# Attention softmax: 1e-9 added to the sums of both heads in one instruction

## The chip, the cores and the metric

The kernel runs on one core of a Trainium2 chip. The metric is the device time of one execution in microseconds (us). A core has five engines with a queue each: TensorE (PE, matrix products; its weight loads are the row PEld), VectorE (DVE), ScalarE (ACT), GpSimd (POOL) and SyncE (SP, which issues transfers). Each works through its queue in order, and they wait for each other by semaphores.

## What is computed

The program is threshold attention followed by a Fourier mixing layer with a two-layer network. The change lies in the attention, for 8 batches of 8 heads with 576 positions of 64 values:

```
scores = scale * q @ k.T
thresh = max(scores) - tau
scores = where(scores >= thresh, scores, -1e9)
attn = exp(scores - max(scores))
attn = attn / (sum(attn) + 1e-09)
out = attn @ v
```

Then, per batch, x is the 576 x 512 matrix of all heads' outputs; u is x plus the real part of its two-dimensional Fourier transform, and the result is u + relu(norm(u) @ w_ch1) @ w_ch2. All of it is in 32-bit floats.

## The kernel before

**Steps.** Two heads make a pair, and a pair is worked in five steps: steps t = 0 to 3 take 128 query rows of each of the two heads, and step t = 4 takes the last 64 rows of both heads together as one block of 128 rows. So a batch has 4 x 5 = 20 steps, the program 160; in 128 of them two blocks are normalized (nh = 2 in the code), in 32 one (nh = 1).

**One step.** `scores` (L431, or L437 for the last step of a pair) puts the products of queries and keys into two score banks `sc`, one for each head; the two banks of a tag rotate, so the next step's products wait for this step's last reader. `softmax` then does, with j as the head:

- L455, DVE: the negated maximum of each row into `neg`
- L463, ACT: exp(score - maximum) into `e`
- L467, ACT, behind the first exponential: the threshold `thr` for both heads
- L471, DVE: `e` times (score >= thr), the masking, which also sums each row into a column of `den`. In the trace it is two entries: the operation, and DVE_READ_ACCUMULATOR, which writes the sum
- L476, DVE: 1e-9 added to that column of `den`
- L485, DVE, after both heads: the inverse of `den`, both columns at once

In the first two batches a copy of the inverse is spread by POOL (L497) and the weighted values are multiplied by it later (L589); from the third batch on, DVE (L488) and ACT (L492) multiply `e` by it, one head each. `weights_in_parts` (L534, L537, L552) transposes `e` on TensorE, ACT copies the result out (L540, L554), and `weighted_values` (L581) multiplies it with v.

**Around it.** In the first 40 steps (two batches) the order of all engines is the order of the program text. In that stretch both weight matrices, given as 64-bit floats, are also loaded in pieces and converted to 32 bits, in stages that the steps call: L297, L300 and L312 on DVE, L305, L308 and L319 on ACT, L317 and L320 on POOL. The hooks `between` (behind the first head's masking; there `weighted_values` of the pair stands, with L589), `meanwhile` (behind the maxima) and `behind` (after both heads; the last conversion stage, on ACT and POOL) place this work inside a step. While little other work is ready, TensorE also runs warming products that feed nothing (`busy`, L112). From the third batch on (step 40) the text orders TensorE alone, and a scheduler orders the other engines.

Two-layer products (L814 and L840 for the first token groups, L918 and L1082 for the later ones), the Fourier products (L684, L701, L705) and their additions fill TensorE between the steps. After step 159, with the last attention done, only these remain.

Of the kernel before, what the change touches and what calls it, by code (L numbers as in the profile page):

```python
# [12 lines left out]
ALU = mybir.AluOpType  # L13
# [15 lines left out]
def _repeated(ap, n):  # L29

    return bass.AP(
        tensor=ap.tensor,
        offset=ap.offset,
        ap=[list(ap.ap[0]), list(ap.ap[1]), [0, n]],
    )
# [12 lines left out]
def kernel(  # L48
# [12 lines left out]
    nc = tc.nc  # L61
# [104 lines left out]
    for u in range(2):  # L166
# [14 lines left out]
        out=q_scale[:], in0=tau_t[:], scalar1=0.0, scalar2=SCALE, op0=ALU.is_ge, op1=ALU.mult  # L181
# [3 lines left out]
        out=below[:], in0=tau_t[:], scalar1=0.0, scalar2=-3.0e38, op0=ALU.is_lt, op1=ALU.mult  # L185
# [3 lines left out]
        out=tau_pos[:], in0=tau_t[:], scalar1=0.0, scalar2=-1.0, op0=ALU.max, op1=ALU.mult  # L189
# [226 lines left out]
    def normalized(n):  # L416


        return n >= 2 * NPAIR
# [23 lines left out]
    def softmax(i, between=None, meanwhile=None, behind=None):  # L443


        t = i % NT
        sc, nh = steps[i]
        neg = sb.tile([128, 2], FP32, tag="neg", bufs=3, name="neg")
        thr = sb.tile([128, 2], FP32, tag="thr", bufs=3, name="thr")
        den = sb.tile([128, 2], FP32, tag="den", bufs=3, name="den")  # L450


        e = sb.tile([128, 2 * S], FP32, tag="e", name="e")
        for j in range(nh):
            nc.vector.tensor_reduce(  # L455
                out=neg[:, j : j + 1], in_=sc[j][:, :, 0:HALF], axis=AXIS_XY, op=ALU.max,
                negate=True,
            )
        if meanwhile is not None:
            meanwhile()  # L460
        for j in range(nh):
            ej = e[:, S * j : S * (j + 1)].rearrange("p (c n) -> p c n", c=2)
            nc.scalar.activation(  # L463
                out=ej, in_=sc[j][:, :, 0:HALF], func=ACT.Exp, bias=neg[:, j : j + 1], scale=1.0
            )
            if j == 0:
                nc.scalar.activation(  # L467
                    out=thr[:, 0:nh], in_=neg[:, 0:nh], func=ACT.Identity,
                    bias=thr_off[:, :], scale=-1.0,
                )  # L470
            nc.vector.scalar_tensor_tensor(  # L471
                out=ej, in0=sc[j][:, :, 0:HALF], scalar=thr[:, j : j + 1], in1=ej,
                op0=ALU.is_ge, op1=ALU.mult, accum_out=den[:, j : j + 1],
            )

            nc.vector.tensor_scalar(  # L476
                out=den[:, j : j + 1], in0=den[:, j : j + 1], scalar1=1e-9, scalar2=None,
                op0=ALU.add,
            )
            if between is not None:  # L480
                between()
                between = None
        if behind is not None:
            behind()
        nc.vector.reciprocal(den[:, 0:nh], den[:, 0:nh])  # L485
        rec = None
        if normalized(i // NT):
            nc.vector.tensor_scalar(  # L488
                out=e[:, 0:S], in0=e[:, 0:S], scalar1=den[:, 0:1], scalar2=None, op0=ALU.mult
            )  # L490
            if nh == 2:
                nc.scalar.activation(  # L492
                    out=e[:, S : 2 * S], in_=e[:, S : 2 * S], func=ACT.Copy, scale=den[:, 1:2]
                )
        else:
            rec = sb.tile([128, 2 * D], FP32, tag="rec", name="rec")
            nc.gpsimd.tensor_copy(  # L497
                rec[:, :].rearrange("p (j d) -> p j d", j=nh), _repeated(den[:, 0:nh], 2 * D // nh)
            )
        if t == 4:  # L500
            nc.scalar.copy(e[:, S : S + 64], e[:, 512:S])
        steps[i] = (e, rec)
# [674 lines left out]
    def step(i):  # L1177
# [15 lines left out]
        if t == 1 and n > 0:  # L1193
            softmax(i, lambda: weighted_values(n - 1, 1), next_stages, last_stage)
            load_v(n + 1)
        elif t == 3:
            softmax(i, lambda: weighted_values(n, 0), next_stages, last_stage)
        else:
            softmax(i, None, next_stages, last_stage)
# [281 lines left out]
```

## Time and profile before

| what | value |
|---|---|
| time, median of three runs | 1632.56 us (1632.07 to 1632.69) |
| span of the profiled execution | 1631.3 us |
| busy PE, PEld | 1583.8 us (97%), 1248.7 us (77%) |
| busy DVE, ACT, POOL | 1173.4 us (72%), 817.8 us (50%), 659.3 us (40%) |
| mean granted TensorE clock | 0.994 of full speed |
| the additions L476 | 288, first at 13.7 us, last at 1431.0 us |
| the first normalization L488 (third batch) | 285.7 us |

A share of busy time is a mean over stages with different limits. The chain of work that ended last says more: it is followed back from the last instruction, at each step to what released it, or to the instruction ahead of it on its engine. In the groups of instructions, a line gives the source line, the engine, the operation, the tile written and those read, the shapes and the count, then the busy time in us and the mean of one in ns, then the engine's idle time just ahead of these and what ended it. In a timeline, a line begins with the start and the duration in us.

### The profile page before, as it was taken

To read this page: it belongs to the slowest core of one execution; us is meant where nothing else is said; L and a number is where in the kernel's file an instruction comes from. 1 tells how busy PE (TensorE), PEld (TensorE's weight loads), DVE (VectorE), ACT (ScalarE), POOL (GpSimd) and SP (SyncE) were. 2 spreads that over 40 slices of the span, in tenths; PEclk is the share of its full clock that TensorE was granted. 3 is DMA by queue.
4 is the path that set the end of the run, shared out by engine and by line. 5 is a ranking of instruction groups with operands and counts; after the bars stand their busy time and mean duration, and the time that the engine had idled before them with its cause. 6 is when DMAs were issued, how large, how long until landed. Compare 5 with 4: busy or idle time off the path is not lost.

```text
span 1631.3 us, 27898 instructions
## 1 busy us (share of the span) xinstructions
PE 1583.8 (97%) x10346; PEld 1248.7 (77%) x10346; DVE 1173.4 (72%) x2518; ACT 817.8 (50%) x1738; POOL 659.3 (40%) x875
## 2 busy tenths in 40 slices
PE   8998999999999999999999999999999999999998
PEld 4555655577887888878888778877878788889998
DVE  7997886667758686857576868786787869664445
ACT  5765665544455454645445546454636455523111
POOL 6784673042421452244342244224352344124332
PEclk9999999999999999999999999999999999999999
DMA  6423222101110101110011010111111110000000
GB/s 162 123 56 113 74 75 57 40 17 22 20 38 17 34 9 43 23 29 16 21 23 36 17 34 11 41 23 35 17 27 32 22 29 2 14 7 7 14 14 14
DMA packets 203084, 57.41 MB, mean 35 GB/s; under 512 B 193827, under 2 KB 193829, under 8 KB 202950
## 3 DMA queue, kind: packets, MB, share of 16 engines
q1 hardware_dynamic: 200438, 55.34, 14.5%
q8 instruction: 82, 1.34, 0.4%
q10 hardware_dynamic: 2512, 0.30, 0.1%
q14 instruction: 52, 0.43, 0.1%
HBM read 46.02 MB, written 9.44 MB: 34 GB/s over the span
## 4 chain that ended last, share of the span: by engine, by line
PE 77%; DVE 14%; ACT 4%; POOL 2%; issue 2%; DMA 1%; SPq 1%; DVEq 0%; ACTq 0%; POOLq 0%
PE ph L918 24%; PE po L1082 20%; PE pv L581 9%; PE sc L431 7%; PE pw L552 6%; PE po L840 3%; DVE neg L455 2%; DVE e L471 2%; PE ph L814 2%; PE sc L437 1%; ACT e L463 1%; PE pn L774 1%; PE py L684 1%; PE pa L701 1%; DVE hs L1043 1%
## 5 line engine op out<-in xcount | busy, mean ns | idle before, releaser
L463 ACT ACTIVATE e<-sc,neg 128x576 f32<-128x576 f32 x288 | 212.5, 738 | 224.7 <-DVE neg L455 224.5
L455 DVE TENSOR_REDUCE neg<-sc 128x1 f32<-128x576 f32 x288 | 207.3, 748 | 161.6 <-PE sc L431 149.7
L471 DVE SCALAR_TENSOR_TENSOR e<-sc,thr,e 128x576 f32<-128x576 f32 x288 | 229.4, 812 | 42.2 <-ACT thr L467 40.4
L1082 PE MATMUL po<-w,hs 128*128 128x256 f32 x1024 | 246.2, 383 | 0.0
L1082 PEld LDWEIGHTS po<-w,hs 128*128 128x128 f32 x1024 | 186.1, 190 | 33.8 <-issue 12.8
L918 PE MATMUL ph<-u_t,w 128*128 128x128 f32 x1536 | 188.1, 277 | 0.0
L431 PE MATMUL sc<-kT,qT 64*128 64x288 f32 x1024 | 174.4, 433 | 12.6 <-DVE e L471 11.1
L918 PEld LDWEIGHTS ph<-u_t,w 128*128 128x128 f32 x1536 | 180.2, 193 | 5.0 <-issue 3.7
L552 PE MATMUL pw<-ident,e 128*128 128x128 f32 x1152 | 170.7, 275 | 7.8 <-ACT y_o L689 2.3
L554 ACT COPY e_t<-pw 128x512 f32<-128x512 f32 x256 | 148.8, 594 | 48.9 <-PE pw L552 48.2
L927 DVE TENSOR_TENSOR hs<-ph,hs 128x512 f32<-128x512 f32 x160 | 106.9, 685 | 70.7 <-PE ph L918 54.0
L431 PEld LDWEIGHTS sc<-kT,qT 64*128 64x128 f32 x1024 | 96.0, 187 | 78.1 <-issue 37.5
L552 PEld LDWEIGHTS pw<-ident,e 128*128 128x128 f32 x1152 | 134.9, 141 | 27.2 <-ACT y_o L689 4.2
L918 PE MATMUL ph<-t_u,s_w 128*128 128x128 f32 x1024 | 126.7, 277 | 2.1 <-POOL t_u L892 1.8
L918 PEld LDWEIGHTS ph<-t_u,s_w 128*128 128x128 f32 x1024 | 119.9, 192 | 7.4 <-issue 4.6
L1082 PE MATMUL po<-hs,s_tile 128*128 128x256 f32 x512 | 121.5, 381 | 0.0
L796 DVE SCALAR_TENSOR_TENSOR u<-po,rstd,u 128x256 f32<-128x256 f32 (+1 forms) x164 | 75.3, 483 | 63.9 <-PE po L1082 62.8
L492 ACT ACTIVATE e<-e,den 128x576 f32<-128x576 f32 x96 | 74.6, 777 | 76.5 <-DVE den L485 76.0
L1082 PEld LDWEIGHTS po<-hs,s_tile 128*128 128x128 f32 x512 | 94.0, 190 | 13.7 <-issue 2.5
L935 ACT ACTIVATE hs<-hs 128x512 f32<-128x512 f32 x112 | 69.2, 630 | 61.6 <-DVE hs L927 61.6
L614 POOL TENSOR_TENSOR half<-x 128x287 f32<-128x287 f32 x48 | 40.5, 865 | 119.5 <-ACT x L587 61.1
L1078 POOL TENSOR_TENSOR hs<-hs,s_tile 128x512 f32<-128x512 f32 x32 | 42.0, 1314 | 107.9 <-PE po L1082 85.0
(194 smaller groups left out, 2899.5 us busy)
## 6 DMA issues: line engine op xcount, KB each, us to landing
hs<-in_moe_w_ch_dram SPq DMA_DIRECT2D x23, 512.0 KB, 4.8
q_in<-in_q_dram SPq DMA_DIRECT2D x128, 72.0 KB, 2.5
out_dram<-u SPq DMA_DIRECT2D x36, 256.0 KB, 2.2
k_in<-in_k_dram SPq DMA_DIRECT2D x124, 72.0 KB, 2.5
v_in<-in_v_dram SPq DMA_DIRECT2D x64, 128.0 KB, 2.4
w<-in_moe_w_ch_dram SPq DMA_DIRECT2D x6, 512.0 KB, 3.6
stage<-in_moe_w_ch_dram SPq DMA_DIRECT2D x3, 512.0 KB, 3.6
v_in<-in_v_dram SPq DMA_DIRECT2D x64, 16.0 KB, 2.2
```

The source lines that it names most:

```text
L431: nc.tensor.matmul(sc[j][:, c, 0:HALF], qT[hp, 128 * t : 128 * t + 128], kT[hp, k0 + HALF * c : k0 + HALF * (c + 1)], start=True, stop=True,)
L455: nc.vector.tensor_reduce(out=neg[:, j : j + 1], in_=sc[j][:, :, 0:HALF], axis=AXIS_XY, op=ALU.max, negate=True,)
L463: nc.scalar.activation(out=ej, in_=sc[j][:, :, 0:HALF], func=ACT.Exp, bias=neg[:, j : j + 1], scale=1.0)
L471: nc.vector.scalar_tensor_tensor(out=ej, in0=sc[j][:, :, 0:HALF], scalar=thr[:, j : j + 1], in1=ej, op0=ALU.is_ge, op1=ALU.mult, accum_out ...
L492: nc.scalar.activation(out=e[:, S : 2 * S], in_=e[:, S : 2 * S], func=ACT.Copy, scale=den[:, 1:2])
L552: nc.tensor.transpose(pw[:, c, :], e[:, c0 : c0 + 128], ident[:, :])
L554: nc.scalar.copy(e_t[:, 4 * j : 4 * j + 4, qs], pw[:, :, :])
L581: nc.tensor.matmul(pv[64 * j : 64 * j + 64, 0:m], vt[:, 2 * c + j, :], e_t[:, 4 * j + c, 0:m] if c < 4 else ends[:, 0, 0:m], start=(c == 0 ...
L796: nc.vector.scalar_tensor_tensor(out=u, in0=product, scalar=self.rstd[:, t : t + 1], in1=u, op0=ALU.mult, op1=ALU.add,)
L918: nc.tensor.matmul(banks[name][:, 128 * q : 128 * q + 128], left[c][:, 512 * part + 128 * q : 512 * part + 128 * q + 128], right[c], start ...
L927: nc.vector.tensor_tensor(out=to, in0=bank, in1=to if other is None else other, op=ALU.add)
L1082: nc.tensor.matmul(bank[:, 0 : DM // 2], left[p], right[p], start=start and p == 0, stop=p == NK - 1, skip_group_check=True,)
```

## The change

The two additions of 1e-9, one behind each head's masking, go. In their place one addition over all `nh` columns of `den` stands behind the hook `behind`, directly ahead of the inverse. It is for having one small instruction of DVE fewer in every step with two heads, and none between the maskings of the two heads. Steps with one head keep one addition.

```diff
@@ in softmax, inside the loop over the heads @@
                 out=ej, in0=sc[j][:, :, 0:HALF], scalar=thr[:, j : j + 1], in1=ej,
                 op0=ALU.is_ge, op1=ALU.mult, accum_out=den[:, j : j + 1],
             )
-
-            nc.vector.tensor_scalar(
-                out=den[:, j : j + 1], in0=den[:, j : j + 1], scalar1=1e-9, scalar2=None,
-                op0=ALU.add,
-            )
             if between is not None:
                 between()
                 between = None
         if behind is not None:
             behind()
+        nc.vector.tensor_scalar(
+            out=den[:, 0:nh], in0=den[:, 0:nh], scalar1=1e-9, scalar2=None, op0=ALU.add
+        )
         nc.vector.reciprocal(den[:, 0:nh], den[:, 0:nh])
```

## The prediction

> **What bounds the kernel now.** I read first the shares of busy time and the chain of work that ended last. TensorE is busy 97% of the span, and the chain says where that is the true bound:
>
> ```profile
> PE 77%; DVE 14%; ACT 4%; POOL 2%; issue 2%; DMA 1%; SPq 1%; DVEq 0%; ACTq 0%; POOLq 0%
> ```
>
> VectorE (DVE) has 14% of the chain, 228 us, so it counts somewhere. Next I cut the span into stretches (columns: length, then busy us of PE, weight loads, DVE, ACT, POOL, then the clock granted to TensorE):
>
> ```profile
> 20.00:140.00 120.00, 111.09 (x578) 64.10 (x577) 110.45 (x243) 83.43 (x170) 82.87 (x101) 0.99 0.47 128
> 140.00:285.00 145.00, 133.31 (x680) 82.41 (x678) 115.55 (x246) 92.52 (x196) 89.91 (x111) 0.96 0.25 58
> ...
> 400.00:600.00 200.00, 197.70 (x1413) 165.35 (x1412) 147.73 (x327) 107.51 (x227) 78.74 (x104) 1.00 0.12 24
> ...
> 1000.00:1200.00 200.00, 197.09 (x1357) 160.91 (x1356) 156.27 (x336) 106.48 (x227) 80.22 (x108) 1.00 0.13 25
> ```
>
> From 20 to 140 us DVE is busy 110.45 of 120 us (92%), and TensorE's 111.09 us contain warming products (L112) that feed nothing: the softmax and weight-conversion chain sets this stretch. From 140 to 285 us DVE is at 80% and the bound changes hands. From 285 to 1435 us TensorE is busy 1134.6 of 1150 us: only 15.4 us could be won there by any means. After 1435 us there is no softmax. So the change must pay before 285 us.
>
> Then the edited instruction, in the groups (count, busy us, mean ns, idle before):
>
> ```profile
> L471 DVE SCALAR_TENSOR_TENSOR e<-sc,thr,e 128x576 f32<-128x576 f32 x288 | 229.4, 812 | 42.2 <-ACT thr L467 40.4 <-ACT e L463 0.6 <-POOL w L377 0.4
> ...
> L476 DVE TENSOR_SCALAR den<-den 128x1 f32<-128x1 f32 x288 | 41.0, 150 | 3.8
> ...
> L485 DVE RECIPROCAL den<-den 128x2 f32<-128x2 f32 x128 | 21.0, 164 | 3.8
> ```
>
> 288 additions of 150 ns, 41.0 us together. Busy time is not the price, though; the order in time of one step with two heads gives it:
>
> ```profile
> 103.19 0.08 DVE L471 DVE_READ_ACCUMULATOR e<-sc,thr,e 128x1 f32 x1
> 103.31 0.15 DVE L476 TENSOR_SCALAR den<-den 128x1 f32<-128x1 f32 x1
> 103.38 0.81 DVE L471 SCALAR_TENSOR_TENSOR e<-sc,thr,e 128x576 f32<-128x576 f32 x1
> ...
> 104.11 0.08 DVE L471 DVE_READ_ACCUMULATOR e<-sc,thr,e 128x1 f32 x1
> 104.23 0.15 DVE L476 TENSOR_SCALAR den<-den 128x1 f32<-128x1 f32 x1
> ...
> 104.42 0.17 DVE L485 RECIPROCAL den<-den 128x2 f32<-128x2 f32 x1
> ```
>
> The first head's addition starts 0.12 us after the read of the accumulator it depends on, and the second head's masking (L471) starts 0.07 us after that, before the addition's recorded end. So from the read to the next masking: 0.19 us. Where the scheduler had put both maskings side by side, the same distance is 0.06 us:
>
> ```profile
> 1019.60 0.08 DVE L471 DVE_READ_ACCUMULATOR e<-sc,thr,e 128x1 f32 x1
> 1019.66 0.82 DVE L471 SCALAR_TENSOR_TENSOR e<-sc,thr,e 128x576 f32<-128x576 f32 x1
> ```
>
> [...] so I price an addition by distances between starts. [...] The trace shows four dips (near 105, 162, 212 and 729 us; 0.53 over 210 to 215 us). On the chain, six score products took 2.25 us at 211 us against 1.20 us elsewhere, eight L814 products 4.72 against 2.85 us, and thirty L918 products 5.24 us at 728 us where 32 take 3.57.
>
> **The change, part by part.**
> - Removed: one addition in each of the 128 steps with two heads (160 steps, of which 32 have one head and keep their addition). In DVE time that is 0.19 - 0.06 = 0.13 us where the addition stood alone between the maskings, 128 x 0.13 = 16.6 us at most if all of it lay on the end. Where the scheduler had filled the wait with another operation, or put both additions together (0.27 us for the pair), what is saved is 0.06 to 0.13 us.
> - Widened: the remaining addition covers two columns. The row has one column only; the nearest bound is the reciprocal, 164 ns for two columns against 145 ns shortest for the group with one. So 0 to 20 ns on 128 steps; I take 0, since a further column costs the masking about (812 - 150) / 575 = 1.2 ns, and keep 20 ns x the 10 to 30 steps that count = 0.2 to 0.6 us for the range.
> - Moved: the addition comes after the second head's masking, with the same wait on it as before, then the reciprocal as before. Behind it wait only the reciprocal, then normalization on DVE and ACT (L488, L492), or the copy of the inverse on POOL (L497). Nothing read the first head's sum early, so no reader waits longer. The second masking starts 0.13 us earlier and frees the second score bank as much earlier.
> - Order elsewhere: the built orders of TensorE and SyncE are the same line for line. On DVE, apart from the additions, one reciprocal and normalization move ahead of a statistics operation; on ACT one normalization moves ahead of one copy (L961), on POOL one pair is swapped. Each is one event below 1 us, beside a TensorE with other work; I take 0.
>
> What lies on the end: I went through the chain in order of time and counted the L476 pieces that stand in front of another head's masking (or in front of the L589 that stands before it). Before 285 us there are 13 (10 of them before 140 us), the later stretches have 6, in places where another DVE operation fills the wait, 0.06 to 0.07 us each. Sum: 13 x 0.13 + 6 x 0.065 = 1.7 + 0.4 = 2.1 us. The other 109 lie beside TensorE products, or beside waits for ACT (L467 makes L471 wait 40.4 us in all), for POOL's weight conversion and for transfers. Forecast: 1632.56 - 2.1 = 1630.5 us.
>
> **The rivals.**
> - B, more of it counts: the chain names one path, but with DVE at 92% the other steps before 285 us are nearly bound as well. From where the chain leaves the first weight transfer (26.6 us) to 285 us there are 29 steps with two heads: 29 x 0.13 = 3.8, plus 0.4: 1628.4 us. For it: DVE's share. Against it: from 43.7 to 56.7 us and in much of 140 to 285 us the chain runs over TensorE, ACT and POOL, where an earlier DVE only waits. If a clock dip also goes, 1.9 us more: 1626.5 us.
> - C, slower: [...] two new dips at the price of the larger one come. At 211 us that dip cost (2.25 - 1.20) + (4.72 - 2.85) = 2.9 us on the chain; 1630.5 + 5.8 = 1636.3 us. For it: gaps of 1.9 us stand in front of the dips at 161, 211 and 728 us. Against it: none of those three gaps has a first-head addition within it, and the three times of before lie within 0.6 us of each other, so the dips hardly vary from run to run.
> - D, nothing: TensorE or POOL takes up every gain as a wait, 1632.5 us. For it: 97% busy TensorE. Against it: the warming products in the early stretch, which are not a bound.
>
> **How the numbers follow.** The forecast has 0.42, B 0.38, C 0.14, D 0.06. The bound of 0.2% is 3.3 us, so faster is below 1629.3 us (B, 0.38), slower above 1635.8 us (C, 0.14), and the forecast and D lie between (0.48). The range goes from 1626.5 (B with a dip gone) to 1634.5 (the forecast with two new dips of the smaller kind, 1630.5 + 2 x 1.9 = 1634.3), and covers the 20 ns of the wider addition. It leaves out most of C and a tail of B.
>
> **What would show it.** After the change the group of the addition has 160 entries, of about 150 ns, 24 us together, and DVE's busy time falls by some 19 us (128 x 0.15). Between two maskings side by side the read of the accumulator is followed in 0.06 us. The end of the second batch, now the first start of L488 at 285.7 us, comes 1.7 us earlier, and the rest of the span is shorter by less than 1 us. If that start moves by 3 us or more, B is right; if it moves by under 0.5 us, D. New stretches with a clock under 0.9 would be C. The forecast is wrong if the gain comes after 285 us, or if the wider addition takes more than 170 ns.

## The result: slower by 3.8 us, and the profile after

The changed kernel takes 1636.06 us (median of 5 runs, 1634.54 to 1636.81) against 1632.3 us for the kernel before, run 5 times beside it. The ratio is 1.0025, 95% interval 1.0013 to 1.0037. The forecast of 1630.5 us had the wrong sign, and the time lies above its range. Below, line numbers of the changed kernel are used: the addition is L480 (before L476), the inverse L483, the normalizations L486 and L490, the copy of the inverse L495.

The changed kernel's shares of busy time, then its chain of waits by engine:

```profile
PE 1582.9 (97%) x10346; PEld 1246.4 (76%) x10346; DVE 1181.8 (72%) x2390; ACT 817.5 (50%) x1738; POOL 660.3 (40%) x875
...
PE 75%; DVE 17%; ACT 4%; issue 2%; POOL 1%; DMA 1%; SPq 0%; DVEq 0%; ACTq 0%; POOLq 0%
```

VectorE lost 128 instructions and is busy for 8.4 us more than before (1173.4 us); its share of the chain rose from 14% to 17%. The groups of the changed kernel, by form (count, busy us, mean ns, idle before), say which instruction took it:

```profile
L480 DVE TENSOR_SCALAR den<-den 128x2 f32<-128x2 f32 x128 | 47.5, 371 | 3.5
...
L483 DVE RECIPROCAL den<-den 128x2 f32<-128x2 f32 x128 | 21.0, 164 | 3.8
...
L480 DVE TENSOR_SCALAR den<-den 128x1 f32<-128x1 f32 x32 | 4.8, 151 | 0.8
```

The 32 additions over one column take 151 ns as before. The 128 over two columns have a mean of 371 ns. The view of the tile `den` adds shortest, median and longest; the first line is of the kernel before, the second of the changed kernel:

```profile
L476 DVE TENSOR_SCALAR den<-den x288: 135/153/156, 13.7 to 1431.0; 128x1 f32<-128x1 f32 x144
```

```profile
L480 DVE TENSOR_SCALAR den<-den x160: 140/168/1428, 14.0 to 1434.6; 128x2 f32<-128x2 f32 x128, 128x1 f32<-128x1 f32 x32
```

The median is 168 ns and the longest 1428 ns, so the mean comes from a minority: counted in the trace, 41 of the 128 take over 0.18 us. Here is one of the first, in the order of time of the changed kernel (start, duration, engine, line):

```profile
17.62 2.12 POOL L229 MEMSET f<- 128x2432 f32 x1
...
18.78 0.08 DVE L471 DVE_READ_ACCUMULATOR e<-sc,thr,e 128x1 f32 x1
18.90 0.87 DVE L480 TENSOR_SCALAR den<-den 128x2 f32<-128x2 f32 x1
19.80 0.17 DVE L483 RECIPROCAL den<-den 128x2 f32<-128x2 f32 x1
19.80 0.29 POOL L495 COPY rec<-den 128x128 f32<-128x128 f32 x1
...
20.15 0.48 PE L535 MATMUL pe<-ident,rec 128*128 128x128 f32 x1 [2.78 <-POOL rec L495]
```

The addition starts 0.12 us after the read of the accumulator, as the additions before did. A memset on GpSimd is running then; it ends at 19.74 us (17.62 + 2.12), and the addition ends at 19.77 us. The inverse behind it, at 19.80 us, waits that long. The copy L495 and TensorE do not wait for this addition, although the profile's chain puts it so: this is the first copy of the program, of the inverse of step 0 (at 14.52 us), and it stands behind the memset in GpSimd's own queue. In the kernel before, the same copy also starts 0.06 us behind the end of the memset, and ahead of the inverse of step 1:

```profile
16.99 2.12 POOL L229 MEMSET f<- 128x2432 f32 x1
...
19.17 0.29 POOL L497 COPY rec<-den 128x128 f32<-128x128 f32 x1
...
19.69 0.17 DVE L485 RECIPROCAL den<-den 128x2 f32<-128x2 f32 x1
```

A second long addition in the changed kernel, 0.6 ms later:

```profile
608.52 1.80 POOL L642 TENSOR_TENSOR f<-f 128x608 f32<-128x608 f32 x1
608.91 1.43 DVE L480 TENSOR_SCALAR den<-den 128x2 f32<-128x2 f32 x1
```

It ends at 610.34 us, 0.02 us behind the GpSimd instruction. Of the 41 long additions, 40 end within 0.06 us of the end of a GpSimd instruction. The other way round it is as sharp: 37 two-column additions started when a GpSimd instruction had been running for 0.02 us or more and had at least 0.18 us to run, and 36 were long. (Of 11 that started within 0.02 us of the GpSimd instruction, 4 were long.) In the kernel before, 108 one-column additions started so, and none was long (longest 156 ns).

So the wider addition waits out what GpSimd is doing. Counting what each long one takes beyond 150 ns, that is 26.9 us in the run, 12.9 us of it (18 additions) before the first normalization, that is the first start of L486. The stretches of the changed kernel, with columns as in the prediction, show whether it counts:

```profile
20.00:140.00 120.00, 109.48 (x555) 63.52 (x556) 107.33 (x215) 82.27 (x165) 83.57 (x102) 0.94 0.42 108
140.00:285.00 145.00, 130.46 (x681) 80.00 (x680) 120.48 (x236) 89.75 (x190) 87.82 (x109) 0.99 0.27 71
...
400.00:600.00 200.00, 197.76 (x1427) 165.58 (x1424) 146.31 (x304) 108.31 (x233) 75.27 (x100) 1.00 0.12 24
...
1000.00:1200.00 200.00, 197.13 (x1361) 160.80 (x1360) 155.80 (x317) 106.65 (x226) 78.70 (x106) 1.00 0.12 24
```

From 20 to 140 us TensorE was busy for 1.61 us less than before, from 140 to 285 us for 2.85 us less; VectorE was busy for 3.12 us less in the first stretch and 4.93 us more in the second. From 400 us on TensorE is as full as before. The chain of waits says by name what stands in the way: before the first normalization it runs through 22 pieces of L480 of 12.1 us together, 11 of them clearly long (the one at 18.90 us, which the chain names wrongly, is among them); before the change it ran through 27 pieces of L476 of 4.3 us. After that only one long addition, of 1.35 us, is on it. A part of it reads (start, us, what):

```profile
33.89 0.02 issue
33.91 1.00 DVE den L480
34.91 0.02 issue
34.94 0.06 DVE den L483
35.00 0.05 issue
35.05 0.55 DVE kT L402
```

So what a held addition delays is VectorE's own queue: here the inverse, then a transposition (L402) that depends on neither.

Put side by side, the same instructions on VectorE and ScalarE start 2.3 us later than before at 22 us, 3.4 at 100, 6.1 at 137 and 5.5 at 290 us (the first normalization: 285.7 before, 291.3 after). The first 2.3 us can't be put down to held additions: the memset ended 0.63 us later than before (19.74 against 19.11 us), the copy of step 0's inverse waited for it, and TensorE's clock was at 0.50 from 20 to 25 us. A run below has the same delay with one-column additions there. The lag later stays between 5.4 and 5.5 us until 724 us and falls to 3.8 us by 775 us; the kernel before had a clock dip at 728 us and this run has none. The profiled spans, 1631.3 and 1634.9 us, differ by what is left.

### The profile page after: what moved, and what is told of

Same layout as the page of the kernel before. It is cut to its first block, busy times and chain, and to the rows that moved or that the text cites. A ratio compares the mean times of both kernels' runs of the same rounds, so it can differ in the third digit from the quotient of the medians.

```text
span 1634.9 us, 27770 instructions
## 1 busy us (share of the span) xinstructions
PE 1582.9 (97%) x10346; PEld 1246.4 (76%) x10346; DVE 1181.8 (72%) x2390; ACT 817.5 (50%) x1738; POOL 660.3 (40%) x875
## 4 chain that ended last, share of the span: by engine, by line
PE 75%; DVE 17%; ACT 4%; issue 2%; POOL 1%; DMA 1%; SPq 0%; DVEq 0%; ACTq 0%; POOLq 0%
PE ph L916 24%; PE po L1080 19%; PE pv L579 8%; PE sc L431 7%; PE pw L550 5%; PE po L838 3%; DVE neg L455 3%; DVE e L471 3%; PE ph L812 2%; PE sc L437 1%; ACT e L463 1%; DVE hs L1041 1%; DVE w L297 1%; PE pn L772 1%; PE py L682 1%
## 5 line engine op out<-in xcount | busy, mean ns | idle before, releaser
L431 PE MATMUL sc<-kT,qT 64*128 64x288 f32 x1024 | 173.8, 434 | 11.6 <-DVE e L471 11.1
L490 ACT ACTIVATE e<-e,den 128x576 f32<-128x576 f32 x96 | 74.5, 776 | 81.3 <-DVE den L483 80.7
```

The source lines that it names most:

```text
L431: nc.tensor.matmul(sc[j][:, c, 0:HALF], qT[hp, 128 * t : 128 * t + 128], kT[hp, k0 + HALF * c : k0 + HALF * (c + 1)], start=True, stop=True,)
L490: nc.scalar.activation(out=e[:, S : 2 * S], in_=e[:, S : 2 * S], func=ACT.Copy, scale=den[:, 1:2])
```

## The experiments

The theory: an addition over two columns is held up by a running GpSimd instruction and one over one column is not, and it costs time only where VectorE sets the pace, in the first 40 steps (the first two batches). The rivals: the new place of the addition, behind the second masking, is to blame; or TensorE's clock dips, set off by the shift (the prediction's rival C).

**The place without the width.** Two one-column additions where the merged one stands:

```diff
-        nc.vector.tensor_scalar(
-            out=den[:, 0:nh], in0=den[:, 0:nh], scalar1=1e-9, scalar2=None, op0=ALU.add
-        )
+        for j in range(nh):
+            nc.vector.tensor_scalar(
+                out=den[:, j : j + 1], in0=den[:, j : j + 1], scalar1=1e-9, scalar2=None,
+                op0=ALU.add,
+            )
```

> The place of the change kept, its width undone: after both maskings two additions of one column each, as many instructions as before. Theory W (the addition over two columns is held up by GpSimd, one over one column never is): no addition over 0.18 us, the first L488 of the third batch at about 284 us (285.7 before, 291.1 after), the time 1629.5 to 1631.5 us. Rival P (the later place, or the clock's dips that it brings, costs the time): additions short, but 1635 to 1637 us as after the change. Rival N (the 3.8 us are the dips' chance alone): anything from 1630 to 1637 us, without a relation to the additions.

Measured: 1632.1 us, ratio 0.9999 (0.9991 to 1.0007). Its tile view:

```profile
L481 DVE TENSOR_SCALAR den<-den x288: 134/150/155, 14.5 to 1427.9; 128x1 f32<-128x1 f32 x144
```

No addition exceeds 155 ns, though 100 of them started beside a GpSimd instruction as counted above, and the loss is gone. The place is not to blame. The time is 0.6 us above the expected range: the place doesn't win anything that shows, either.

**The width without the place.** The kernel before, where the second head's addition covers both columns (the first head's sum so gets 1e-9 twice):

```diff
+            c0 = 0 if j == 1 else j
             nc.vector.tensor_scalar(
-                out=den[:, j : j + 1], in0=den[:, j : j + 1], scalar1=1e-9, scalar2=None,
+                out=den[:, c0 : j + 1], in0=den[:, c0 : j + 1], scalar1=1e-9, scalar2=None,
```

> The kernel before with both additions where they were, but in steps with two heads the second one covers both columns (the first head's sum gets 1e-9 twice). The width alone. W: some 40 of 128 wide additions end about 25 ns behind a GpSimd instruction and take up to 1.4 us, the time 1635 to 1638 us. P: 1632 to 1633 us, as before. N: no relation.

Measured: 1640.28 us, ratio 1.0046 (1.0032 to 1.0060). Its groups by form:

```profile
L477 DVE TENSOR_SCALAR den<-den 128x2 f32<-128x2 f32 x128 | 49.9, 390 | 3.6
...
L477 DVE TENSOR_SCALAR den<-den 128x1 f32<-128x1 f32 x160 | 23.8, 149 | 2.1
```

47 additions were long, by 29.4 us in all, 25 of them before the first normalization, which starts at 292.6 us. Width alone, in the old place and with the old number of instructions, brings the whole loss and more. It is more than the 1635 to 1638 us expected; more additions were held early than in the changed kernel (25 against 18), and why is open.

**Two columns in another form.** The changed kernel, its two-column addition written with an accumulator output into a spare column:

```diff
@@ steps with two heads; those with one keep the plain form; the rest of the edit is left out @@
-            out=den[:, 0:nh], in0=den[:, 0:nh], scalar1=1e-9, scalar2=None, op0=ALU.add
+            out=den[:, 0:2], in0=den[:, 0:2], scalar1=1e-9, scalar2=0.0, op0=ALU.add,
+            op1=ALU.add, accum_out=spare[:, :],
```

> The changed kernel with the addition over two columns at its new place, in the form that also writes a sum over its columns (to a scratch column nobody reads), which is an operation and a read of the accumulator. The width is that of the change; only the form differs. W[...]: no addition over 0.2 us and 1631 to 1633 us, since a read of 0.08 us is added to each. If it is two columns as such[...]: the additions are held up as after the change and the time is 1636 us or more.

Measured: 1631.9 us, ratio 0.9995 (0.9987 to 1.0003). A step in its order of time:

```profile
32.18 1.30 POOL L320 TENSOR_TENSOR w<-w,hs 128x512 f32<-128x512 f32 x1
...
32.52 0.15 DVE L482 TENSOR_SCALAR_CACHE_REDUCE den<-den 128x2 f32<-128x2 f32 x1
32.60 0.08 DVE L482 DVE_READ_ACCUMULATOR den<-den 128x1 f32 x1
32.72 0.17 DVE L490 RECIPROCAL den<-den 128x2 f32<-128x2 f32 x1
```

The addition starts 0.34 us into a GpSimd instruction of 1.30 us, and takes 0.15 us. In the changed kernel the same step, beside the same instruction:

```profile
33.58 1.30 POOL L320 TENSOR_TENSOR w<-w,hs 128x512 f32<-128x512 f32 x1
...
33.91 0.99 DVE L480 TENSOR_SCALAR den<-den 128x2 f32<-128x2 f32 x1
```

Of 41 two-column additions of the accumulator form that started so, none was held (longest 157 ns). So it is not two columns as such, but this form of instruction over two columns. The reciprocal over two columns isn't held either: in the changed kernel 29 started so, and the longest of all took 168 ns. Together: held were 36 of 37 (two columns), 0 of 108 and 0 of 100 (one column), 0 of 41 (accumulator form). Why the plain addition over two columns waits and these forms don't is not shown, and no run tries three columns.

**Where it counts.** Two-column additions in the first 40 steps alone, one-column ones after; and the opposite, which has `i >= 2 * per_batch` in the condition:

```diff
-        nc.vector.tensor_scalar(
-            out=den[:, 0:nh], in0=den[:, 0:nh], scalar1=1e-9, scalar2=None, op0=ALU.add
-        )
+        if i < 2 * per_batch:
+            nc.vector.tensor_scalar(
+                out=den[:, 0:nh], in0=den[:, 0:nh], scalar1=1e-9, scalar2=None, op0=ALU.add
+            )
+        else:
+            for j in range(nh):
+                nc.vector.tensor_scalar(
+                    out=den[:, j : j + 1], in0=den[:, j : j + 1], scalar1=1e-9, scalar2=None,
+                    op0=ALU.add,
+                )
```

> The changed kernel, with the addition over two columns only in the first 40 steps (the stretch before the third batch); from the third batch on two additions of one column each at the same place. W, with the part that all of the loss lies where VectorE sets the pace: 1635 to 1637.5 us, as the whole change, though the later stretches held 23 of the 41 long additions and 14.0 of 26.9 us of their holding. If the later ones count by their length: 1632.5 to 1634 us.

> The reverse: two additions of one column each in the first 40 steps, the addition over two columns from the third batch on. W: some 23 long additions remain in the trace, up to 1.4 us each, and the time is that of the narrow one, 1631 to 1633 us, since TensorE is busy over 98% there. If the later ones count by their length: 1634 to 1636 us.

Measured: 1638.13 us, ratio 1.0033 (1.0021 to 1.0046), with two columns early; 1631.49 us, 0.9993 (0.9984 to 1.0001), with two columns late. Their two-column groups, early first:

```profile
L481 DVE TENSOR_SCALAR den<-den 128x2 f32<-128x2 f32 x32 | 16.7, 522 | 1.1
```

```profile
L481 DVE TENSOR_SCALAR den<-den 128x2 f32<-128x2 f32 x96 | 29.6, 308 | 2.4
```

17 long additions with 11.6 us over 150 ns cost the whole loss early (the time is 0.6 us above the expected range); 24 long ones with 14.0 us cost nothing that shows late. The late ones stand where TensorE is full (in the changed kernel busy for 197.76 of the 200 us from 400 us on).

**Without the addition.** The maximum of each row contributes exp(0) = 1, so every sum is at least 1; by arithmetic alone, neighbouring 32-bit floats are 2^-23, or 1.2e-7, apart there, and 1e-9 rounds away. This kernel leaves the addition out:

```diff
-        nc.vector.tensor_scalar(
-            out=den[:, 0:nh], in0=den[:, 0:nh], scalar1=1e-9, scalar2=None, op0=ALU.add
-        )
```

> The addition of 1e-9 is left out altogether, so this is the ceiling of any change to it. W: 1.5 to 4 us faster than before, 1628.5 to 1631 us, since what the additions cost on the end is some 0.13 to 0.3 us in the 20 to 30 steps of the first stretch that count. P and N: the same, or no relation.

Measured: 1626.42 us (1625.49 to 1627.63), ratio 0.9965 (0.9952 to 0.9977), the fastest of all: 6.3 us below the 1632.71 us of the kernel before in that comparison, which is more than expected. The end of a step in its order of time:

```profile
31.87 0.07 DVE L471 DVE_READ_ACCUMULATOR e<-sc,thr,e 128x1 f32 x1
...
31.98 0.17 DVE L480 RECIPROCAL den<-den 128x2 f32<-128x2 f32 x1
```

From the read of the last accumulator to the inverse it is 0.11 us; before it was 0.31 us (104.11 to 104.42 us in the prediction's lines). The addition costs 0.20 us there, as a link between two dependent instructions. The first normalization starts at 281.7 us, 4.0 us earlier than before. That fits the chain of the kernel before: L476 has 4.3 us on it up to there and 1.3 us behind, 5.6 us together, against the 6.3 us measured.

**Are the clock dips needed?** In the first profile of the changed kernel the held addition at 18.90 us stands beside a TensorE gap of 2.78 us and a clock of 0.50 from 20 to 25 us. I took the gap for the work of the hold, as the chain has it; the copy that ends it waits for the memset, as shown above. Two more warming products in step 1 fill the gap, to see whether the dip goes with it; the changed kernel was run again beside it.

```diff
-            busy(2 if i < NCHUNK else 1)
+            busy(4 if i == 1 else 2 if i < NCHUNK else 1)
```

> The changed kernel, with two warming products more (some 2 us of TensorE work that feeds nothing) in step 1, in front of the transposes that wait there for the inverse held up by the addition of 18.9 us. It fills TensorE's gap of 2.8 us ahead of the first clock dip. If that dip is a part of the loss that the held addition brings about: no clock under 0.9 in the first 30 us, and 1 to 2 us faster than the change, 1634 to 1635.5 us. If the dip costs nothing or comes anyway by chance: 1636 to 1637 us.

> The changed kernel once more, on the chip and against the runs of before of this group, as the measure for the other three. W: 1635 to 1638 us, some 40 additions that end about 25 ns behind a GpSimd instruction, at much the same places before 285 us as in the first trace. N (chance of the dips): a time within 1 us of before is possible.

Measured: 1635.04 us with the warming products, ratio 1.0016 (1.0010 to 1.0023); 1635.72 us for the changed kernel, 1.0020 (1.0012 to 1.0029). The first 30 us of each, clock granted in the third column from the end, warming first:

```profile
0.00:30.00 30.00, 26.92 (x101) 13.33 (x102) 21.14 (x47) 14.55 (x26) 20.98 (x66) 1.00 0.72 179
```

```profile
0.00:30.00 30.00, 25.50 (x99) 12.75 (x100) 20.57 (x47) 14.86 (x27) 20.73 (x66) 1.00 0.75 183
```

The clock is full in both, so this run of the changed kernel had no early dip even without the edit, and what the warming does for the dip is not answered: the two ratios overlap. But something else is. The changed kernel without an early dip is still slower, with 40 long additions, 16 of them early (11.7 us over 150 ns), and a first normalization at 288.6 us. The dip at 20 us isn't needed for the loss. Up to 285 us the mean clock of this run is 0.99, that of the kernel before 0.98.

Nor does the dip need a held addition. In the run with two columns late, whose additions there are over one column, the same copy starts at 19.98 us, behind a memset that ends at 19.92 us; TensorE's gap is 2.95 us, the clock falls as well (0.66 from 20 to 25 us), and the work at 25 us is 1.9 us later than before. Its first 30 us:

```profile
0.00:30.00 30.00, 24.53 (x86) 12.68 (x88) 18.11 (x48) 13.59 (x25) 19.83 (x66) 0.94 0.71 178
```

So the early delay and dip of the first profile belong to that execution. In the repeated run, without them, the first normalization comes 2.9 us later than before, not 5.6.

## Why the prediction was wrong

- **What bounds the kernel.** This held: the first 285 us are where VectorE's time counts. The two runs with the width early or late show it on both sides, +5.4 us and -1.1 us by their ratios.
- **Widened: 0 to 20 ns, taken as 0.** This step failed. I priced two columns by the reciprocal of the same width (164 ns) and a further column by the masking (1.2 ns), that is by other operations, and asked only for the length of an instruction left alone; GpSimd doesn't occur in this term. Left alone the two-column addition does take 168 ns; but its mean is 371 ns, 221 ns more than the 150 ns I took, 128 x 0.221 = 28.3 us of VectorE's time. What of it reaches the end is read best between kernels that do the rest alike: 1635.72 us for the changed kernel run again, 1631.49 us with one column at a time in the first 40 steps. That is 4.2 us where the prediction allowed 0.2 to 0.6, and the first comparison gives as much (ratios of 1.0025 and, at the same place with one column, 0.9999). On the chain before the first normalization the additions grew by more, from 4.3 to 12.1 us (11.9 us in the second profile), but the chain counts what was on it, not what would have held the work up in its place. The prediction named the reading that would refute it, more than 170 ns, and that is the one that came.
- **The sign was in the profile of before.** Its tile view has the normalization, the same kind of instruction over 576 columns:

```profile
L488 DVE TENSOR_SCALAR e<-e,den x120: 469/521/1569, 285.7 to 1431.3; 128x576 f32<-128x576 f32 x120
```

  A median of 521 and a longest of 1569 ns: a spread by three for the same work, where the one-column addition keeps within 135 to 156 ns. It is the same hold: 31 of the 120 took over 0.56 us, and 28 of these ended 0.31 to 0.32 us behind the end of a GpSimd instruction; of 17 that started with at least 0.56 us of one to run, all were long. I read the mean of the edited row, which had no spread to show.
- **Removed: 2.1 us.** A gain in this direction exists, its size is not settled. The kernel closest to the forecast is the accumulator form, one unheld two-column instruction: by its ratio 0.8 us faster, interval from 2.1 us faster to 0.5 us slower. The first normalization came 1.1 us earlier in it and 1.7 us earlier with two one-column additions at the new place, but 0.8 us later (286.6 us) in the run with two columns late, whose first 40 steps are the same as those of the latter: single profiles don't settle 2 us. VectorE's busy time, forecast to fall by 19 us, rose by 8.4 us for the reason above.
- **Order and readers: 0.** This held as far as the runs show: the two one-column additions at the new place lose nothing (ratio 0.9999).
- **Rival C** named 1636.3 us, near what came, for another reason. Its dips did move (the changed kernel's first profile has 0.50 from 20 to 25 us and 0.52 from 115 to 120 us, and none near 728 us), and what sets one off is not shown. But the repeated run lacks the early dip and loses all the same, and the run with two columns late has that dip without a held addition. The argument against C, three times within 0.6 us, was wrong in itself: over 25 and 40 runs the kernel before spreads over 1630.5 to 1634.7 and 1631.0 to 1635.4 us.

## What to carry to other kernels

Before two small VectorE operations are merged into a wider one, ask whether the wider form can still run beside GpSimd as its parts could, and what GpSimd runs at that moment; here 128 instructions fewer took 8.4 us more of the engine. Price an operation that the trace doesn't show by the same kind of instruction and its shortest, median and longest, not by another kind of the same width: a spread by three in a row was here the mark of an instruction that is held up. And where the chain names a releaser, look at what the waiting engine itself was doing: the first held addition seemed to delay a copy that stood behind a memset in its own queue. Look first, though, for an operation that can go altogether: an addition that rounds away stood between two dependent instructions in every step, and leaving it out won more than any way of placing it.

## What was unexpected of the hardware

- A held addition ends 22 to 30 ns behind the end of the GpSimd instruction (40 of the 41 in the first profile), and a memset, which reads no tile, holds as well (L229; the addition beside it runs from 18.90 to 19.77 us). Two columns are enough for it.
- One exception: a two-column addition beside L391, a `tensor_scalar` of GpSimd, took 168 ns in the changed kernel; the run with two columns early and the one with more warming had one such case each at the same place. Why this one doesn't hold is open.
- Single executions of an unchanged kernel spread by 4 us. In the profiled runs the places of the clock dips vary, and the lag of the first profile moves by 1.6 us where the kernel before has a dip and it has none (5.4 to 3.8 us at 728 us).
